# Order of the opening's loads, products without a reader, and query loads two pairs sooner in an attention and two-stage MLP kernel

## The chip, the cores and the metric

The kernel runs on one core of a Trainium2 chip. The metric is the device time of one execution in microseconds (us). TensorE (PE) multiplies, VectorE (DVE), ScalarE (ACT) and GpSimd (POOL) work on what it leaves in PSUM and on data in SBUF, and SyncE (SP) hands out the DMA transfers.

## The reference

What is computed, cut to what matters: attention of 2 batches with 8 heads, 576 positions and 64 elements a head, where a small network of the relative position adds a bias to the scores, then two stages of matrix products on the 1152 rows that come out.

```python
scores = scale * np.matmul(q, k.transpose(0, 1, 3, 2))
rel = (pos[:, None] - pos[None, :]).astype(np.float32)
psi_rel = np.log1p(np.abs(rel))
psi_i = np.log1p(np.maximum(pos[:, None].astype(np.float32), 1.0))
h = np.maximum((psi_rel / psi_i)[..., None] @ w1 + b1, 0.0)   # 32 hidden
scores = scores + (h @ w2).transpose(2, 0, 1)[None, :, :, :]  # 8 heads
attn = softmax(scores);  x = attn @ v          # x: 1152 x 512
x = ((x @ w_a) * (x @ w_b)) @ w_out            # 512 -> 1536 -> 512
h = x @ w_in                                   # 512 -> 1024
solu = h * softmax(h)
out = (layernorm(solu) * g_ln) @ w_out2        # 1024 -> 512
```

The weights of the two later stages come as float64 and are read as pairs of 32-bit words.

## The kernel before

**Units and pairs.** The attention part goes over nine units of 128 rows of scores: units 0 to 7 are four blocks of 128 positions, each for batch 0 and batch 1, and unit 8 holds the last 64 positions of both batches. A unit has four pairs of heads, so the main loop (lines 614 to 682) runs over 36 pairs, m = 0 to 35, and some steps more to drain. In the turn of pair m PE makes the scores of both its heads (`scores`, L399), then DVE adds the bias and takes the minimum row by row (`biased`, L413: `tensor_tensor_reduce`, shown in the trace as `CUSTOM_DVE_ANT_0 e<-s,bias`; two of them make a pair), ACT takes the exponents (L420), POOL multiplies with the reciprocal of the sum (`shares`, L435). PE transposes the result two pairs later (L441, L452) and multiplies it with the values in the turn after (`values`, L484, into the tile `xx`). At the end of a unit ACT and DVE split `xx` into a high and a low part (`xhi`, `xlo`, L495) for the products of the next stage. Engines run their instructions in the order in which the code issues them; the schedule is written out by hand.

**Queries.** The queries of unit u + 2 are loaded by `fetch` (L257) into a tile `nat_q`, one load for heads 0 to 3 and one for heads 4 to 7 (each two DMA issues, four in unit 8), in pairs p = 2 and p = 3 of unit u (last lines of the loop). The query of the next unit is turned by PE in each pair (`turn`, L276), into the tile of scores `spare` that the second head of the pair has just been given. ACT and DVE read it into `qhi` and `qlo` (L309, L318). For unit 8, POOL clears the tiles ahead of that (`clear_q`, L283), in unit 6's last pair and in unit 7's second.

**Bias.** The bias is made in 36 groups of 16 rows, T = 0 to 35. For each, ACT and DVE make four tiles of relus from a table (`bias_hidden`, L361 and L363; who makes which is the table `HIDDEN`), PE sums them over the hidden elements (`bias_sums`, L371, 16 products into a PSUM tile `bps`), ACT scales the sums into the tile `st` (`bias_out`, L381) and SP sends `st` to the bias tile of the block (L383), of which eight groups make one for 128 rows. Groups 0 to 8 are made ahead of the loop (`N0` is 8), group m + 9 in pair m of the loop.

**Opening.** PE makes the right part of the relu table from `psi_r` (`table`, L207), the offsets of the relus (L214) and the scales of the outputs (L227), then the loop over T = 0 to 7 begins. In it PE also turns the queries of unit 0 and the keys of batch 0 (`piece`, L276; a key piece goes to PSUM as `xx`, `tp_k` or a tile of the scores' pool, and ACT and DVE split it into `khi`, `klo`). The left part of the table is made in T = 6. The keys of a batch come in five pieces through an area `arena`; those of batch 1 are turned in pairs 0, 1 and 2 of the loop.

**Queue.** All loads and the bias transfers stand in SP's queue, in the order of the code. An issue takes SP's time, and a transfer that waits for its data holds up all that stand behind it.

**After.** From pair 28 on the words of the first weights of the next stage are loaded and converted between the attention's last pairs (`first_one`: words, ACT's `single` at L94), and from there PE works on the next stages to the end.

The loads of the opening and of the loop are these lines:

```python
for w in ks[1][:3]:
    fetch(w)
for p in range(-1, 2):
    load_v(0, p)
for w in ks[1][3:]:
    fetch(w)
...
if now and p > 1 and u + 2 < NU:
    fetch(("q", u + 2, p - 2, 0))
```

## Time and profile before

| | us |
|---|---|
| median of 3 runs | 536.64 (536.34 to 538.48) |
| the profiled execution | 536.58 |
| its span in the trace | 534.5 |
| TensorE (PE) busy | 504.0 (94%) |
| VectorE (DVE) busy | 401.3 (75%) |
| ScalarE (ACT) busy | 285.2 (53%) |
| GpSimd (POOL) busy | 143.7 (27%) |

The span runs from the first to the last instruction of the profiled execution; what lies around it is 2.1 us. The busy times are sums over the whole program, in which the attention part with its many small steps (until about 200 us) and the large matrix products behind it differ, so they are read by stretch. A row of the time line gives the start, the duration, the engine (SPq: SP's queue, with the time in which it handed out the issues), the line of the kernel, the operation, what it writes and reads, the shape and how many instructions of that kind follow each other. A bracket says how long the engine sat idle before the row and which engine, tile and line released it.

### The profile page before, as it was taken

Reading aid. Unit: us, or ns where it says so; the run is one execution under the profiler, and the core shown is the slowest. Engines: PE = TensorE matmul, PEld = TensorE weight load, DVE = VectorE, ACT = ScalarE, POOL = GpSimd, SP = SyncE. Lnnn points to the kernel's source line nnn. Section 1 sums busy time; section 2 is a strip of 40 time slices with the busy share of each in tenths; the row PEclk is TensorE's granted clock in tenths of the full one; section 3 lists DMA queues with packets and bytes.
Section 4 is the critical chain, followed back from the end, with each engine's and each line's share of the span. In section 5 each row is a group of like instructions: output and inputs, shape, how many; then the busy total and the mean of one; then the engine's idle time right before and its main releaser. Section 6 shows DMA issues by size and latency. Waiting matters only on the chain.

```text
span 534.5 us, 13462 instructions
## 1 busy us (share of the span) xinstructions
PE 504.0 (94%) x5416; PEld 446.1 (83%) x5416; DVE 401.3 (75%) x873; ACT 285.2 (53%) x617; POOL 143.7 (27%) x216
## 2 busy tenths in 40 slices
PE   7848899999979999999999999999999999999997
PEld 3436777877767799999999999999999988888886
DVE  4848899999967943887998898897875466666561
ACT  5847899999978732655564344422535332322221
POOL 2003333344356740322222122242225230000000
PEclk9968999999999999999999999999999999999999
DMA  5886654444653103535543353353300000000011
GB/s 133 196 174 149 155 115 109 94 105 110 149 135 120 42 2 108 172 121 155 158 155 122 118 157 119 119 158 119 120 0 1 1 0 21 20 21 20 25 35 39
DMA packets 63520, 51.74 MB, mean 97 GB/s; under 512 B 41182, under 2 KB 53731, under 8 KB 63460
## 3 DMA queue, kind: packets, MB, share of 16 engines
q1 hardware_dynamic: 63184, 50.88, 35.1%
q8 instruction: 42, 0.69, 0.5%
q14 instruction: 18, 0.15, 0.1%
q10 hardware_dynamic: 276, 0.02, 0.0%
HBM read 36.73 MB, written 2.36 MB: 73 GB/s over the span
## 4 chain that ended last, share of the span: by engine, by line
PE 74%; DVE 8%; ACT 7%; DMA 5%; issue 4%; SPq 1%; POOL 1%; DVEq 0%; ACTq 0%
PE pm L128 27%; PE po L128 14%; PE py L922 9%; PE ph L862 9%; PE bps L371 5%; PE xx L484 3%; DVE h L363 3%; ACT e L420 3%; DMA nat_q<-in_q_dram 2%; DVE e L413 2%; PE pl L903 1%; PE s L399 1%; PE pt L452 1%; DMA words<-in_moe_w_out_dram 1%; ACT qhi L309 1%
## 5 line engine op out<-in xcount | busy, mean ns | idle before, releaser
L128 PE MATMUL pm<-xhi,abh 128*128 128x384 f32 x240 | 80.2, 334 | 0.0
L128 PE MATMUL pm<-xhi,abl 128*128 128x384 f32 x240 | 80.2, 334 | 0.0
L128 PE MATMUL pm<-xlo,abh 128*128 128x384 f32 x240 | 80.2, 334 | 0.0
L98 POOL TENSOR_SCALAR f<-f 128x512 f32<-128x512 f32 x48 | 41.4, 862 | 141.8 <-ACT f L94 117.3
L435 POOL TENSOR_SCALAR e<-e,rec 128x576 f32<-128x576 f32 x72 | 53.4, 754 | 62.9 <-DVE rec L430 52.2
L420 ACT ACTIVATE e<-e,nm 128x576 f32<-128x576 f32 x72 | 55.9, 776 | 22.4 <-DVE nm L413 11.4
L413 DVE CUSTOM_DVE_ANT_0 e<-s,bias 128x576 f32<-128x576 f32 x72 | 53.7, 747 | 13.8 <-DMA arena<-in_k_dram 5.4
L371 PE MATMUL bps<-h,w2bd 128*32 128x288 f32 x576 | 48.2, 438 | 11.1 <-DVE h L363 6.5
L363 DVE TENSOR_SCALAR h<-tabs 128x576 f32<-128x576 f32 x106 | 48.5, 514 | 1.0 <-PE bps L371 0.8
L128 PE MATMUL po<-gh,oh 128*128 128x384 f32 x144 | 48.5, 337 | 0.6 <-DVE x2s L793 0.6
L128 PE MATMUL po<-gh,ol 128*128 128x384 f32 x144 | 48.4, 336 | 0.0
L128 PE MATMUL po<-gl,oh 128*128 128x384 f32 x144 | 48.4, 336 | 0.0
L128 PEld LDWEIGHTS pm<-xhi,abh 128*128 128x128 f32 x240 | 45.1, 188 | 0.0
L128 PEld LDWEIGHTS pm<-xlo,abh 128*128 128x128 f32 x240 | 45.1, 188 | 0.0
L128 PEld LDWEIGHTS pm<-xhi,abl 128*128 128x128 f32 x240 | 45.1, 188 | 0.0
L110 DVE SCALAR_TENSOR_TENSOR f<-words,f 128x512 int32<-128x512 int32 x48 | 42.9, 895 | 1.6
L147 ACT COPY one<-pm 128x384 f32<-128x384 f32 x36 | 17.2, 479 | 50.2 <-PE pm L128 50.2
L94 ACT ACTIVATE f<-words 128x512 f32<-128x512 f32 x48 | 32.4, 676 | 18.3 <-DMA words<-in_moe_w_out_dram 7.6
L484 PE MATMUL xx<-et,vsb 128*32 128x128 f32 (+1 forms) x1280 | 40.1, 267 | 0.0
L371 PEld LDWEIGHTS bps<-h,w2bd 128*32 128x32 f32 x576 | 20.0, 114 | 23.4 <-issue 8.8
L877 ACT ACTIVATE ev<-ph,small 128x512 f32<-128x512 f32 x18 | 12.2, 684 | 49.7 <-DVE small L874 49.7
L484 PEld LDWEIGHTS xx<-et,vsb 128*32 128x32 f32 x1280 | 34.1, 111 | 5.5 <-issue 0.2
(151 smaller groups left out, 1223.7 us busy)
## 6 DMA issues: line engine op xcount, KB each, us to landing
bias<-st SPq DMA_DIRECT2D x40, 288.0 KB, 3.6
words<-in_moe_w_out_dram SPq DMA_DIRECT2D x20, 512.0 KB, 3.5
words<-in_moe_w_a_dram SPq DMA_DIRECT2D x12, 512.0 KB, 3.5
words<-in_moe_w_b_dram SPq DMA_DIRECT2D x12, 512.0 KB, 3.7
nat_q<-in_q_dram SPq DMA_DIRECT2D x32, 128.0 KB, 3.5
words<-in_moe_w_in_dram SPq DMA_DIRECT2D x8, 512.0 KB, 3.6
arena<-in_k_dram SPq DMA_DIRECT2D x16, 128.0 KB, 4.4
vsb<-in_v_dram SPq DMA_DIRECT2D x16, 128.0 KB, 3.7
```

The costliest lines, as they stand in the source:

```text
L94: nc.scalar.activation(f, words[:, :, 1].bitcast(F32), AF.Abs)
L98: engine.tensor_scalar(f, f, WORD_MAX, WORD_MIN, op0=ALU.min, op1=ALU.max)
L110: nc.vector.scalar_tensor_tensor(out=b, in0=words[:, :, 0], scalar=29, in1=b, op0=ALU.logical_shift_right, op1=ALU.bitwise_or)
L128: nc.tensor.matmul(ps, w, x, start=(i == 0), stop=(i == n - 1))
L363: nc.vector.tensor_scalar(h, win, sc, 0.0, op0=ALU.add, op1=ALU.max)
L371: nc.tensor.matmul(bps[32 * qd:32 * qd + 32, a, 0:SH], w2bd, h[:, a * SH:(a + 1) * SH], start=True, stop=True)
L413: nc.vector.tensor_tensor_reduce(out=halves(e), in0=ps[:, :, 0:SH], in1=halves(bias_t[it][:, h, :]), op0=ALU.add, op1=ALU.min, scale=1.0, ...
L420: nc.scalar.activation(e, e, AF.Exp, bias=nm, scale=-1.0, accum_out=sums[:, h:h + 1])
L435: nc.gpsimd.tensor_scalar(e, e, rec[:, h:h + 1], 1.0, op0=ALU.mult, op1=ALU.mult)
L484: nc.tensor.matmul(px[rows, p, cols], lhsT, rhs, start=(c == 0 and m == 0), stop=(c == NC), skip_group_check=True)
L862: nc.tensor.matmul(ph[u][:, a], x[:, kc, cols], w[:, kc, a * 512:(a + 1) * 512], start=(i == 0), stop=(i == 3 * KD - 1))
L922: nc.tensor.matmul(ps, x[:, c, :], w[:, c, cols], start=(i == 0), stop=(i == 3 * KF - 1))
```

## The change

- The first bias group after which the loop starts, T = 9, gets its relus ahead of the loop and not in pair 0.
- Unit 1's queries, batch 1's keys and batch 0's values are loaded behind the transfer of T = 8 (the ninth); before, the queries stood ahead of T = 5 and the rest ahead of T = 8.
- A function `beside` issues products whose result nobody reads: 5, 2 and 2 of 128 columns in the opening, and 2 of 512 columns ahead of the first scores.
- The left part of the table is made in T = 5 and not T = 6, in a tile of the scores' pool, and ACT copies both its halves; before DVE did.
- The queries of unit u + 2 are loaded in pairs 0 and 1 of unit u.
- In the loop the key pieces of pairs 0 to 2 are turned ahead of the bias sums of the pair.
- The tile `xx` becomes two tiles, one for each parity of the unit; a key piece in it is split by two copies of half the size.
- The clears of unit 8's query tiles take the half that no query is written to.

```diff
-        xx = ps_x.tile([P, 2, 512], F32, tag="x", name="xx")
+        xx = [ps_x.tile([P, 512], F32, tag=f"x{r}", name=f"xx{r}") for r in range(2)]
+        def beside(n, ps, x):
+            for _ in range(n):
+                nc.tensor.matmul(ps, ident, x, start=True, stop=True)
...
+        warm_ps = ps_t.tile([P, 2, 512], F32, tag="t", name="warm_ps")
+        beside(5, warm_ps[:, 0, 0:P], ident)
         halves_r = table(half, UW - half, psi_r, half - 12, ps_s, "s")
...
+        beside(2, warm_ps[:, 0, 0:P], ident)
         nc.scalar.copy(*halves_r[0])
...
         scales()
+        beside(2, warm_ps[:, 0, 0:P], ident)
...
-                    nc.gpsimd.memset(t_.bitcast(F32), 0.0)
+                    nc.gpsimd.memset(t_[:, :, ROWS[1 - m]].bitcast(F32), 0.0)
...
+            if (u, h) == (0, 0):
+                beside(2, ps[:, 0], tb[:, UW - 512:UW])
...
-                st_["x", u] = xx[:, u % 2].rearrange("p (a t) -> p a t", a=HP)
+                st_["x", u] = xx[u % 2].rearrange("p (a t) -> p a t", a=HP)
...
-            if T == N0 - 2:
-                halves_l = table(low, half - low, psi_l, low - 12, ps_t, "t")
+            if T == N0 - 3:
+                halves_l = table(low, half - low, psi_l, low - 12, ps_s, "s")
+                for half_l in halves_l:
+                    nc.scalar.copy(*half_l)
...
-            if T == N0 - 3:
-                for g in range(2):
-                    fetch(("q", 1, g, 0))
         assert done is None and len(order) == 3
-        for half_l in halves_l:
-            nc.vector.tensor_copy(*half_l)
         bias_hidden(N0)
         bias_sums(N0 - 1)
         bias_out(N0 - 1)
-        for w in ks[1][:3]:
-            fetch(w)
-        for p in range(-1, 2):
-            load_v(0, p)
-        for w in ks[1][3:]:
-            fetch(w)
-        for p in range(2, HP):
-            load_v(0, p)
...
         bias_out(N0)
+        for w in [("q", 1, 0, 0)] + ks[1][:4] + [("q", 1, 1, 0)] + ks[1][4:]:
+            fetch(w)
+        for p in range(-1, HP):
+            load_v(0, p)
+        bias_hidden(N0 + 1)
...
-            if m == 0:
-                bias_hidden(T)
...
+            made = [piece(w, room) for w, room in zip(keys_at.get(m, []), "xt")]
             if T is not None:
                 bias_sums(T)
-            made = [piece(w, room) for w, room in zip(keys_at.get(m, []), "xt")]
...
-            if now and p > 1 and u + 2 < NU:
-                fetch(("q", u + 2, p - 2, 0))
+            if now and p < 2 and u + 2 < NU:
+                fetch(("q", u + 2, p, 0))
```

SP's queue at the end of the opening, before: `nat_q_1_0` and `nat_q_1_1` are unit 1's queries, `arena` takes the keys of batch 1, `vtl` and `vsb` the values of batch 0, and `st_5` to `st_9` are the bias groups of these numbers.

```order
L257 DMA nat_q_1_0_340<-in_q_dram 128x4x64 x2
L257 DMA nat_q_1_1_343<-in_q_dram 128x4x64 x2
L383 DMA bias_0_208<-st_5_363 16x8x576
L383 DMA bias_0_208<-st_6_392 16x8x576
L383 DMA bias_0_208<-st_7_414 16x8x576
L262 DMA arena_163<-in_k_dram 128x4x64 x4
L269 DMA arena_163<-in_k_dram 32x4x64 x4
L336 DMA vtl_162<-in_v_dram 64x4x64 x2
L338 DMA vsb_161<-in_v_dram 128x4x64 x4
L262 DMA arena_163<-in_k_dram 128x4x64 x4
L338 DMA vsb_161<-in_v_dram 128x4x64 x4
L383 DMA bias_1_486<-st_8_487 16x8x576
```

The same place of SP's queue now:

```order
L399 DMA bias_0_219<-st_7_419 16x8x576
L399 DMA bias_1_471<-st_8_472 16x8x576
L266 DMA nat_q_1_0_475<-in_q_dram 128x4x64 x2
L271 DMA arena_174<-in_k_dram 128x4x64 x4
L278 DMA arena_174<-in_k_dram 32x4x64 x4
L271 DMA arena_174<-in_k_dram 128x4x64 x2
L266 DMA nat_q_1_1_488<-in_q_dram 128x4x64 x2
L271 DMA arena_174<-in_k_dram 128x4x64 x2
L352 DMA vtl_173<-in_v_dram 64x4x64 x2
L354 DMA vsb_172<-in_v_dram 128x4x64 x8
L399 DMA bias_1_471<-st_9_572 16x8x576
L266 DMA nat_q_2_0_589<-in_q_dram 128x4x64 x2
```

All loads that stood ahead of T = 8 stand behind it, queries and keys ahead of the values, and unit 2's first queries follow T = 9.

SP's queue in the last units, before: `nat_q_8_0` and `nat_q_8_1` are unit 8's queries, `st_33` to `st_35` the last bias groups, `words_0` the first weights of the next stage.

```order
L257 DMA nat_q_7_1_2834<-in_q_dram 128x4x64 x2
L383 DMA bias_4_2820<-st_33_2925 16x8x576 x2
L383 DMA bias_4_2820<-st_34_3022 16x8x576 x2
L383 DMA bias_4_2820<-st_35_3121 16x8x576 x2
L257 DMA nat_q_8_0_3127<-in_q_dram 64x4x64 x4
L257 DMA nat_q_8_1_3222<-in_q_dram 64x4x64 x4
L90 DMA words_0_3306<-in_moe_w_a_dram 128x4x256
```

And now:

```order
L399 DMA bias_4_2842<-st_33_2944 16x8x576 x2
L266 DMA nat_q_8_0_2957<-in_q_dram 64x4x64 x4
L399 DMA bias_4_2842<-st_34_3046 16x8x576 x2
L266 DMA nat_q_8_1_3059<-in_q_dram 64x4x64 x4
L399 DMA bias_4_2842<-st_35_3150 16x8x576 x2
L90 DMA words_0_3325<-in_moe_w_a_dram 128x4x256
```

The two query loads each stand two bias groups sooner, and T = 35 is now the last ahead of the words.

DVE at the end of unit 0, with what its instructions wait for, before: `xlo` is the low part of the unit's result, `h_0` and `h_2` are relus, `nm` and `e` belong to the pair's bias step.

```order
L466 COPY et_1_1221<-pt_1_1175 128x8x64 [waits DVE_49,PE_49]
L318 SCALAR_TENSOR_TENSOR qlo_1_0_1058<-s_7_1148,qhi_1_0_1057 128x128 [waits Activation_49]
L495 TENSOR_TENSOR xlo<-xx,xhi 128x4x128 [waits PE_49]
L363 TENSOR_SCALAR h_0_1231<-tabs 128x576 [waits DVE_49]
L363 TENSOR_SCALAR h_2_1235<-tabs 128x576 [waits DVE_49]
```

And now:

```order
L484 COPY et_1_1243<-pt_1_1197 128x8x64 [waits DVE_49,PE_49]
L334 SCALAR_TENSOR_TENSOR qlo_1_0_1083<-s_7_1170,qhi_1_0_1082 128x128 [waits Activation_49]
L513 TENSOR_TENSOR xlo<-xx_104,xhi 128x4x128
L379 TENSOR_SCALAR h_0_1253<-tabs 128x576 [waits DVE_49]
L379 TENSOR_SCALAR h_2_1257<-tabs 128x576 [waits DVE_49]
```

`xlo` stands at the same place in DVE's order and has lost its wait for PE.

## Rows read from the trace of the kernel before

**Rows 1.** Busy time by stretch: us; PE, PEld, DVE, ACT, POOL; clock; DMA; GB/s

```profile
30.00:35.00 5.00, 1.96 (x14) 1.17 (x15) 2.99 (x9) 3.18 (x7) 0.00 (x0) 0.50 0.44 94
155.00:160.00 5.00, 2.29 (x36) 1.88 (x37) 1.97 (x7) 1.42 (x5) 3.46 (x7) 0.84 0.51 101
200.00:300.00 100.00, 99.39 (x730) 98.57 (x730) 79.76 (x131) 50.94 (x98) 21.32 (x26) 1.00 0.44 138
```

**Rows 2.** Time line (start, duration), PE and DVE in pairs 28 to 30

```profile
155.09 0.75 DVE L413 CUSTOM_DVE_ANT_0 e<-s,bias 128x576 f32<-128x576 f32 x1
...
158.00 0.84 PE L276 MATMUL s<-ident,nat_q 64*128 64x64 f32 x4 [2.56 <-DMA nat_q<-in_q_dram]
...
158.87 0.76 DVE L413 CUSTOM_DVE_ANT_0 e<-s,bias 128x576 f32<-128x576 f32 x1 [2.95 <-PE s L276]
...
162.58 0.76 DVE L413 CUSTOM_DVE_ANT_0 e<-s,bias 128x576 f32<-128x576 f32 x1 [1.71 <-PE s L399]
...
162.83 0.29 PE L276 MATMUL s<-ident,nat_q 64*128 64x64 f32 x4
...
165.48 0.76 DVE L413 CUSTOM_DVE_ANT_0 e<-s,bias 128x576 f32<-128x576 f32 x1 [0.17 <-PE s L399]
```

**Rows 3.** Time line of SP's queue ahead of pair 28

```profile
143.75 8.98 SPq L383 DMA_DIRECT2D bias<-st  x6
152.83 6.14 SPq L257 DMA_DIRECT2D nat_q<-in_q_dram  x8
```

**Rows 4.** Time line, ACT and PE in pairs 30 and 31

```profile
165.89 0.72 ACT L94 ACTIVATE single<-words 128x512 f32<-128x512 f32 x1
...
170.36 0.28 PE L441 MATMUL s<-ident,e 64*128 64x64 f32 x2 [1.15 <-POOL e L435]
```

**Rows 5.** Time line, DVE in pair 4

```profile
56.41 0.76 DVE L413 CUSTOM_DVE_ANT_0 e<-s,bias 128x576 f32<-128x576 f32 x1 [1.76 <-PE s L276]
```

**Rows 6.** Time line, SP's queue and PE around pair 8

```profile
67.86 1.10 SPq L257 DMA_DIRECT2D nat_q<-in_q_dram  x2
...
73.22 0.34 PE L276 MATMUL s<-ident,nat_q 64*128 64x64 f32 x4 [0.95 <-DMA nat_q<-in_q_dram]
```

**Rows 7.** Time line, DVE and ACT at a unit's end; DVE's waits, 50 to 215 us

```profile
88.28 0.69 DVE L495 TENSOR_TENSOR xlo<-xx,xhi 128x512 fp32r<-128x512 f32 x1 [0.47 <-PE xx L484]
...
90.60 0.78 ACT L420 ACTIVATE e<-e,nm 128x576 f32<-128x576 f32 x1
...
DVE xlo L495 <- PE xx L484: 2.8, 6, 0.5
```

**Rows 8.** Time line, PE and ACT to 11 us; L371's products (ns least/median/most)

```profile
2.43 2.53 PE L207 MATMUL table<-psi_r 1*32 1x346 f32 x16 [2.43 <-DMA psi_r<-in_w_dram]
...
6.94 2.91 PE L371 MATMUL bps<-h,w2bd 128*32 128x288 f32 x16 [0.41 <-DVE h L363]
...
9.99 0.74 ACT L381 ACTIVATE st<-bps,rp 128x576 f32<-128x576 f32 x1 [1.21 <-PE bps L371]
...
L371 PE MATMUL bps<-h,w2bd x16: 660/687/689, 6.9 to 9.2; 128*32 128x288 f32 x16
...
L371 PE MATMUL bps<-h,w2bd x65: 406/406/431, 12.8 to 20.0; 128*32 128x288 f32 x65
```

**Rows 9.** Time line, ACT, DVE and PE in pairs 0 to 2

```profile
24.46 0.74 ACT L381 ACTIVATE st<-bps,rp 128x576 f32<-128x576 f32 x1
...
31.02 0.76 DVE L413 CUSTOM_DVE_ANT_0 e<-s,bias 128x576 f32<-128x576 f32 x1 [5.35 <-DMA arena<-in_k_dram]
...
36.13 0.69 PE L276 MATMUL xx<-ident,arena 64*128 64x64 f32 x8
...
39.37 0.75 DVE L413 CUSTOM_DVE_ANT_0 e<-s,bias 128x576 f32<-128x576 f32 x1
...
45.56 2.10 PE L371 MATMUL bps<-h,w2bd 128*32 128x288 f32 x16
```

**Rows 10.** The page's DMA issues: count, KB each, median us from issue to landing

```profile
arena<-in_k_dram SPq DMA_DIRECT2D x16, 128.0 KB, 4.4
```

More of the change, by code (lines that the diff above doesn't have):

```diff
@@ L275, in turn @@
                 for r in rows:
[L276 removed]
+                    nc.tensor.transpose((ps[r] if ps is xx else ps[:, r])[:, at + i * HF:at + (i + 1) * HF], nat[ROWS[r], h].rearrange("p s d -> p (s d)"), ident[ROWS[r], ROWS[r]])
         def room_q(u, g, m):
@@ L297, in k_views @@
         def k_views(b, g, c, ps, at):
+            if ps is xx:
+                turned = [t_[:, at:at + HG * HF] for t_ in xx]
+                if c < NK:
+                    heads = slice(g * HG, (g + 1) * HG)
+                    return [(*(t_[:, b, heads, c * P + r * HF:c * P + (r + 1) * HF] for t_ in (khi, klo)), turned[r].rearrange("p (h t) -> p h t", h=HG)) for r in range(2)]
+                hi, lo = (t_[:, b, :, NK * P:SH].rearrange("p (g i) t -> p i g t", g=2) for t_ in (khi, klo))
+                return [(hi, lo, turned[b].rearrange("p (i g t) -> p i g t", i=HG, g=2))]
             turned = ps[:, :, at:at + HG * HF]
```

5 lines of the change are left out of this document (2 added, 3 removed).

## The prediction

> **What bounds the kernel now.** First the busy times by stretch [rows 1]: columns are the busy time of each engine in the stretch, then the granted clock, the DMA share, GB/s. From 200 us on TensorE (PE) is full, and the work there only waits for the attention part to end; a microsecond saved before 200 us ends the program a microsecond sooner. So the forecast is a sum over places ahead of that where something waits. The time line then gives them: a row's bracket says how long its engine sat idle and who ended it. Five places touch the change: the last units [rows 2 to 4], pair 4 [rows 5], pair 8 [rows 6], the unit boundaries [rows 7], and the opening [rows 8 to 10]. Pairs of heads are counted m = 0 to 35, T counts the groups of 16 bias rows; fast pairs in between are bound by VectorE (DVE) or ScalarE (ACT), nothing of which changes.
>
> **The last units, the largest term.** Pair 28 needs the queries of unit 8 on PE, in the same tile of scores that DVE reads next. DVE starts the pair at 155.09 and should start its second half about 0.76 us later; it sat idle 2.95 us and began at 158.87, because PE waited 2.56 us for nat_q [rows 2]. The transfer is late because it is issued late: SP handed out both query loads of unit 8 in one go from 152.83, behind the last bias transfers [rows 3]. The change issues the first of them two pairs, some 8 us, sooner, right behind T = 33, the first of the three groups that SP handed out from 143.75 [rows 3]: from about 144.85 us, two issues later at 0.55 us (two took 1.10, [rows 6]). Its own four issues and the 5.36 us that such a load took from issue to PE's start there (67.86 to 73.22) put it at about 152, 3 us before it is needed. So the wait goes entirely, not in part. [...] From PE's query transposes to the next pair's first DVE row took 158.00 to 162.58 = 4.58 us there, but 162.83 to 165.48 = 2.65 us one pair later, with the clock back. Without the wait the transposes stand at 155.4, the next pair begins at 155.4 + 2.65 = 158.05 and not at 162.58: 4.5 us. Late next would be DVE or ACT with the pair's own work; but pair 29, with the same work, ran from 162.58 to 165.48 = 2.9 us on all engines together, and 155.09 + 2.9 is 158.0 too.
>
> Then GpSimd (POOL): the clears of the last queries, four each time, are halved. The second time they stand ahead of the shares for which PE waited 1.15 us [rows 4]. That wait is the most that this can give, nothing the least, if a clear's fixed part rules; I take 0.5. The words of the first weights are the counterweight: they now wait for the landing of T = 35's bias, issued just before 152.83 [rows 3], near 157 by the 4.4 us of a key load [rows 10], and land as much later, near 161.4; ACT took them up at 165.89 [rows 4], which comes 4.5 us sooner, at 161.4. It costs nothing by this count and up to 1.1 us if they land late. **Last units: -5.0 (from -3.9 to -5.6).**
>
> **Pair 4.** The same wait: DVE idle 1.76 us for the transposes of unit 2's queries [rows 5]. They were fetched in pair 2 and are now in pair 0, behind T = 9's transfer; in SP's order that comes after 26 loads, from about 26.2 us on (below) at 0.55 us each, so near 41, and they land by 47 for a need at 56.41 - 1.76 = 54.65. Nothing else stands late there: DVE's relus follow at once. **-1.8 (from -1.6 to -2.0).**
>
> **Pair 8.** PE waited 0.95 us [rows 6], but DVE was behind by only part of that; I take half. **-0.45 (0 to -0.95).** Later boundaries show no such wait, so for pairs 9 to 27 the sooner loads are worth nothing.
>
> **Unit boundaries.** The change splits the tile xx in two. DVE's xlo no longer waits for PE's next products: 0.47 us before it [rows 7], six times. But ACT is as full there: its next exponent at 90.60 shows no idle time before it, so most of a DVE gain runs into ACT. I take 0.11 of the 0.47, six times. **-0.7 (0 to -2.8).**
>
> **The opening, first part.** The clock of the first microseconds is read from the products themselves: the first sixteen products of the bias sums took 687 ns each, from 12.8 us on the same took 406 [rows 8]. So it is at the lower level until somewhere near 10 to 12 us. Nine idle products are added there. Price: the table's products, two rounds of 346 columns, took 2.53 us; 128 columns are 2.53 / 2 x 128 / 346 = 0.47 us at that level, 0.28 at the upper by 406 / 687. Five start when the identity exists, by my estimate a microsecond ahead of the table's 2.43, and end at 1.4 + 5 x 0.47 = 3.75: 1.3 us late. Four more are 1.9 us, less the 0.41 that PE idled before the first sums: the worst case is 1.3 + 1.9 - 0.4 = +2.8. The best is set by ACT, which idled 1.21 us before its first output [rows 8] and hardly at all in the ten microseconds after: -1.2, if the products raise the clock by about 6 us. I take **+0.4**, below the middle, since PE then works without a break from 1.4 us instead of 2.4.
>
> [...]
>
> **The opening, second part.** ACT's last outputs: two copies of the left table come to ACT from DVE, each narrower than half an output (0.74 us, [rows 9]), so under 0.37, and half of the two in idle time; so T = 8's output, ended at 24.46 + 0.74 = 25.20, ends at 25.55. Now SP: unit 1's queries, keys and the values stood ahead of T = 5 to 8 and share the rings with them; DVE began its first pair only at 31.02, after 5.35 us idle on a DMA [rows 9]; the row names a key load, but the first pair reads the bias, and T = 7's transfer is the last of it. The groups' outputs follow each other at 1.8 us (T = 0 at 9.99, T = 8 at 24.46), so T = 7 is out at 25.2 - 1.8 = 23.4, and in the changed order, with nothing foreign ahead, lands near 27.8 by a key load's 4.4 us; then the first half of pair 0 starts near 28.3, when the scores are done; the two long idle products ahead of them (four times 0.28 each at the upper level) lie in PE's wait. But the second half needs unit 1's queries, now issued behind T = 8: 25.6 + 0.6 = 26.2, and 5.36 us to PE's start as above: 31.55, against 31.02 + 0.7 = 31.7 before. Equal. Four key loads follow at 0.55 us each; the last, issued at 28.9, lands 4.4 us later [rows 10]: 33.3. PE then turns the keys (0.69 for the first eight of sixteen at the lower clock, some 1.1 in all) and sums T = 9 (2.10 at that clock). From the end of the sums, at 36.1, where the key turns began, to DVE's next pair it took 39.37 - 36.1 = 3.3 before: 33.3 + 1.1 + 2.1 + 3.3 = 39.8 against 39.37 [rows 9]. The relus of T = 9, moved ahead, are out of the way in both counts. The clock was 0.50 in 30 to 35 us [rows 1] after PE had idled; PE idles as long now. Pairs 1 and 2 give this back, since their key turns now stand in PE's wait for a free score buffer. The second part: **0 (from -1.7, if the clock stays up, to +1.5, if keys land at 5.5 us)**. DVE's saved copies count for nothing, since DVE then waits anyway.
>
> **Sum.** -5.0 - 1.8 - 0.45 - 0.7 + 0.4 + 0 = -7.55 us. The profiled execution took 536.58 us (span 534.5 and 2.1 around it), the median of the runs is 536.64: the same for this purpose. 536.58 - 7.55 = **529.0 us**. All ends together would be 522.3 and 535.4.
>
> **Rivals.** First, the opening pays: products at the lower level without raising it, keys late. +2.8 and +1.5 for +0.4 and 0: 532.9 us. For it: PE is the first engine to work there, and ACT, behind it, has no slack. Against: ACT's idle 1.21 us. 0.16. Second, the clock: up from 6 us and never down around 30 us: -1.2 and -1.7 for +0.4 and 0: 525.7. Against: PE still has little to do between 29 and 33 us. 0.12. Third, the last units find a new bound, the words or POOL, and give 2.5 instead of 5.0: 531.5. For: the words wait for one more transfer. 0.14. Fourth, the sooner loads are issued but held in SP's queue behind bias transfers, and pairs 28 and 4 wait as before: the last units keep 0.5 and pair 4 nothing: 529.0 + 4.5 + 1.8 = 535.3. Against: the order puts them four transfers further ahead. 0.05. Fifth, slower: 26 loads behind T = 8 on eight completion lanes, each issue waiting for the load eight before it. At 4.4 us it holds (26 / 8 x 4.4 = 14 us, done by 40; the values are wanted only after 45.56, [rows 9]). From about 9 us a landing it decides: keys at 47 and not 41, each later pair behind; at 10 us the keys of pairs 0, 1 and 2 come 5.6 us late each in turn, some 11 us in all: 540 us. Nothing in the trace lands so late; 4.4 is the keys' median. 0.03.
>
> **How the numbers follow.** The forecast has 0.50. A measurement of this kernel tells 0.5%, 2.7 us, from no change: the line lies at 533.9. The forecast, the second and third rival and nearly all of the first lie below: faster 0.90. The fourth and the first's tail: same 0.07. The fifth: slower 0.03. The range 525.3 to 533.0 takes in the first and third rival's centres and half of the second, and leaves 2 in 10 out.
>
> **What would show it.** In the changed trace: no idle bracket from nat_q at PE in pairs 4, 8 and 28, and no clock under 1.00 near 158 us; pair 28 to 29 about 3 us long, pair 32 some 5 us nearer to pair 28 than before; no wait before xlo; the first output of the bias near 10 us; DVE's first pair near 28.3 and pair 1 within 1.5 us of 39.4. It is wrong if SP shows the query loads of unit 8 still issued after T = 35, if ACT waits for words in pair 29, or if pair 1 begins after 41 us.

## The result and the profile after

The changed kernel takes **531.53 us** (median of 5 runs, 530.36 to 532.78) against 536.64 us before, so 5.1 us less; over all runs of both the ratio is 0.9895, 95% interval 0.9864 to 0.9926. That is in the range and on the side that was forecast (529.0; 525.3 to 533.0). The profiled executions are 531.99 and 536.58 us, 4.6 us apart; their spans are 530.2 and 534.5, 4.3 us apart, and it is in these that the steps are compared. Where the time went and where it came back is read from the start of each pair's bias step on VectorE. The table has the start of the pair's first row, before and after, out of the time line.

| pair | before | after | difference |
|---|---|---|---|
| 0 | 31.02 | 31.12 | +0.10 |
| 1 | 39.37 | 41.50 | +2.13 |
| 3 | 50.07 | 52.39 | +2.32 |
| 4, second half | 56.41 | 56.89 | +0.48 |
| 9 | 76.91 | 77.19 | +0.28 |
| 27 | 151.88 | 151.35 | -0.53 |
| 29 | 162.58 | 157.40 | -5.18 |
| 31 | 168.88 | 165.69 | -3.19 |
| 32 | 175.27 | 171.01 | -4.26 |
| 35 | 185.67 | 181.42 | -4.25 |

The opening loses 2.1 to 2.3 us and pair 4 gives 1.85 back. From there to pair 9 it is another 0.2, and from pair 9 to 27, with the unit boundaries, 0.8. Pair 28 gives 4.6; pair 29 takes 0.35 and pair 30 1.6 of it; pair 31 gives 1.1. From pair 35 to the end both take the same 348.8 us.

**The last units.** The time line of SP's queue in the changed kernel (start, time of the issues, line, what is loaded, count), answering to [rows 3]:

```profile
143.22 1.17 SPq L399 DMA_DIRECT2D bias<-st  x2
144.49 2.66 SPq L266 DMA_DIRECT2D nat_q<-in_q_dram  x4
147.25 2.11 SPq L399 DMA_DIRECT2D bias<-st  x2
149.46 2.65 SPq L266 DMA_DIRECT2D nat_q<-in_q_dram  x4
152.21 1.83 SPq L399 DMA_DIRECT2D bias<-st  x2
157.38 0.37 SPq L90 DMA_DIRECT2D words<-in_moe_w_a_dram  x1
```

Unit 8's first queries are issued at 144.49 and not at 152.83. VectorE, pairs 28 to 32 of the changed kernel, answering to [rows 2], and the clock of the same stretch as in [rows 1]:

```profile
154.56 0.75 DVE L431 CUSTOM_DVE_ANT_0 e<-s,bias 128x576 f32<-128x576 f32 x1
155.31 0.74 DVE L431 CUSTOM_DVE_ANT_0 e<-s,bias 128x576 f32<-128x576 f32 x1
157.40 0.76 DVE L431 CUSTOM_DVE_ANT_0 e<-s,bias 128x576 f32<-128x576 f32 x1
...
160.65 0.76 DVE L431 CUSTOM_DVE_ANT_0 e<-s,bias 128x576 f32<-128x576 f32 x1 [0.34 <-PE s L417]
...
165.69 0.74 DVE L431 CUSTOM_DVE_ANT_0 e<-s,bias 128x576 f32<-128x576 f32 x1
...
171.01 0.74 DVE L431 CUSTOM_DVE_ANT_0 e<-s,bias 128x576 f32<-128x576 f32 x1
```

```profile
155.00:160.00 5.00, 4.91 (x134) 4.18 (x130) 4.53 (x15) 4.29 (x14) 3.79 (x8) 1.00 0.47 135
```

Pair 28's second half follows the first at once, pair 29 comes 2.84 us after pair 28 (7.49 before), and the granted clock is 1.00 where it was 0.84 (before, it is 0.50 from 158.35 to 161.76 us, just behind TensorE's wait for nat_q, and 1.00 after that). But from pair 30 to 31 it is now 5.04 us, where it was 3.40. ScalarE and TensorE there, answering to [rows 4]:

```profile
162.54 0.68 ACT L94 ACTIVATE single<-words 128x512 f32<-128x512 f32 x1 [1.51 <-issue]
165.13 0.40 PE L417 MATMUL s<-khi,qhi 64*128 64x288 f32 x2 [1.51 <-DVE qlo_True L334]
```

ScalarE stands idle 1.51 us ahead of the first words of the next stage ("issue": nothing that the profile shows ended the wait), and what stands behind on it, pair 30's exponent and the split of the queries, is late by as much for TensorE. Pair 31 itself takes 5.32 us and not 6.39, since TensorE's wait for POOL's shares [rows 4] is gone.

**The opening.** TensorE to 12 us in the changed kernel, then ScalarE's first and last output (answering to [rows 8, 9]):

```profile
1.35 2.50 PE L176 MATMUL warm_ps<-ident 128*128 128x128 f32 x10 [1.35 <-POOL ident masks.py:199]
3.78 2.53 PE L212 MATMUL table<-psi_r 1*32 1x346 f32 x16
...
6.73 1.22 PE L176 MATMUL warm_ps<-ident 128*128 128x128 f32 x4
...
8.43 1.22 PE L176 MATMUL warm_ps<-ident 128*128 128x128 f32 x4
9.58 2.05 PE L387 MATMUL bps<-h,w2bd 128*32 128x288 f32 x16
```

```profile
11.87 0.74 ACT L397 ACTIVATE st<-bps,rp 128x576 f32<-128x576 f32 x1 [1.11 <-PE bps L387]
...
27.05 0.78 ACT L397 ACTIVATE st<-bps,rp 128x576 f32<-128x576 f32 x1
```

The nine short products take 4.9 us of TensorE (2.50 + 1.22 + 1.22), the sums start at 9.58 and not at 6.94, the first output at 11.87 and not at 9.99, and T = 8's at 27.05 and not at 24.46. Behind it, around pair 0:

```profile
28.40 1.98 PE L176 MATMUL s<-tabs,ident 128*128 128x512 f32 x4 [1.52 <-DVE klo L330]
...
32.78 0.34 PE L285 MATMUL s<-ident,nat_q 64*128 64x64 f32 x4 [1.40 <-DMA nat_q<-in_q_dram]
```

The two long products wait for the scores' buffer and then hold the first scores for 1.98 us; the second half of pair 0 waits for unit 1's queries until 32.78 in any case (e2 below).

### The profile page after: what moved, and what is told of

Read it like the earlier page. It is cut to its first block, busy times and chain, and to the rows that moved or that the text cites. A ratio compares the mean times of both kernels' runs of the same rounds, so it can differ in the third digit from the quotient of the medians.

```text
span 530.2 us, 13526 instructions
## 1 busy us (share of the span) xinstructions
PE 508.7 (96%) x5438; PEld 449.1 (85%) x5438; DVE 400.3 (76%) x874; ACT 285.3 (54%) x622; POOL 142.4 (27%) x216
## 3 DMA queue, kind: packets, MB, share of 16 engines
q1 hardware_dynamic: 63184, 50.88, 35.1%
## 4 chain that ended last, share of the span: by engine, by line
PE 72%; ACT 11%; DVE 7%; issue 5%; DMA 3%; SPq 1%; POOL 1%; DVEq 0%; ACTq 0%; POOLq 0%
PE pm L128 27%; PE po L128 14%; PE py L932 10%; PE ph L872 10%; ACT e L438 4%; DVE h L379 4%; PE bps L387 3%; PE xx L502 3%; ACT st L397 2%; PE pl L913 1%; PE s L417 1%; ACT qhi L325 1%; ACT h L377 1%; DMA words<-in_moe_w_out_dram 1%; DVE qlo L334 1%
## 5 line engine op out<-in xcount | busy, mean ns | idle before, releaser
L387 PE MATMUL bps<-h,w2bd 128*32 128x288 f32 x576 | 49.3, 434 | 2.0 <-DVE nm L431 2.0
L110 DVE SCALAR_TENSOR_TENSOR f<-words,f 128x512 int32<-128x512 int32 x48 | 42.5, 886 | 1.6
L502 PE MATMUL xx<-et,vsb 128*32 128x128 f32 (+1 forms) x1280 | 42.2, 263 | 0.0
L502 PEld LDWEIGHTS xx<-et,vsb 128*32 128x32 f32 x1280 | 35.6, 110 | 6.1 <-issue 0.2
L109 DVE SCALAR_TENSOR_TENSOR f<-words,f 128x512 int32<-128x512 int32 x48 | 34.5, 719 | 1.3
```

The source lines that it names most:

```text
L109: nc.vector.scalar_tensor_tensor(out=b, in0=words[:, :, 1], scalar=-0x40000000, in1=b, op0=ALU.bitwise_and, op1=ALU.bitwise_or)
L110: nc.vector.scalar_tensor_tensor(out=b, in0=words[:, :, 0], scalar=29, in1=b, op0=ALU.logical_shift_right, op1=ALU.bitwise_or)
L387: nc.tensor.matmul(bps[32 * qd:32 * qd + 32, a, 0:SH], w2bd, h[:, a * SH:(a + 1) * SH], start=True, stop=True)
L502: nc.tensor.matmul(px[rows, p, cols], lhsT, rhs, start=(c == 0 and m == 0), stop=(c == NC), skip_group_check=True)
```

## The experiments

The times, in us. The ratio refers to runs of the kernel before that were timed beside each kernel (their medians are 536.64, 536.97, 537.13 and 537.31). The last columns are starts of VectorE's pairs in the profiled execution, and the time from pair 30 to 31.

| kernel | median (range) | ratio, 95% | pair 1 | pair 27 | 30 to 31 | pair 35 |
|---|---|---|---|---|---|---|
| changed | 531.53 (530.36 to 532.78) | 0.9895 [0.9864, 0.9926] | 41.50 | 151.35 | 5.04 | 181.42 |
| e1 no short products | 530.58 (530.30 to 532.19) | 0.9887 [0.9870, 0.9905] | 39.40 | 150.04 | 4.85 | 179.93 |
| e2 no long products | 532.21 (531.79 to 533.78) | 0.9917 [0.9900, 0.9934] | 41.34 | 150.83 | 5.37 | 181.20 |
| e3 none of them | 530.10 (529.63 to 531.74) | 0.9880 [0.9861, 0.9898] | 39.48 | 149.60 | 5.82 | 180.44 |
| e12 first two only | 530.65 (529.28 to 531.61) | 0.9862 [0.9810, 0.9915] | 39.54 | 148.76 | 4.47 | 178.25 |
| e4 before, queries | 531.29 (530.84 to 531.68) | 0.9897 [0.9880, 0.9914] | 39.45 | 150.65 | 3.36 | 180.17 |
| e7 e4 and xx in two | 530.21 (528.58 to 531.58) | 0.9868 [0.9841, 0.9895] | 38.72 | 148.42 | 3.23 | 178.14 |
| e6 e7 and half clears | 530.01 (527.51 to 531.02) | 0.9864 [0.9831, 0.9896] | 39.23 | 148.28 | 3.21 | 176.91 |
| e11 e6, one load later | 529.51 (528.32 to 530.91) | 0.9842 [0.9799, 0.9885] | 39.51 | 149.40 | 3.04 | 177.90 |
| e5 words taken later | 532.92 (531.80 to 533.38) | 0.9917 [0.9895, 0.9940] | 41.30 | 151.39 | 5.52 | 181.81 |
| e8 e3 and e5 | 531.01 (530.88 to 531.52) | 0.9887 [0.9863, 0.9910] | 39.68 | 149.55 | 5.14 | 179.61 |
| e9 fetches moved | 529.73 (529.22 to 531.72) | 0.9854 [0.9793, 0.9916] | 40.37 | 150.58 | 3.09 | 179.10 |
| e10 one load later | 530.57 (529.22 to 531.18) | 0.9859 [0.9808, 0.9911] | 40.37 | 151.15 | 4.64 | 180.70 |

The intervals of nearly all of them overlap, so the times alone rank few; what a step costs is read from the pairs.

### The products that nobody reads: e1, e2, e3, e12

Theory: the short ones cost what they take and bring no clock; the long ones stand in a wait. Rival: they pay by the clock.

e1:

```diff
-        beside(5, warm_ps[:, 0, 0:P], ident)
...
-        beside(2, warm_ps[:, 0, 0:P], ident)
...
-        beside(2, warm_ps[:, 0, 0:P], ident)
```

> The changed kernel without the nine products of 128 columns ahead of the first bias sums (nobody reads their result). Theory: they cost more than the clock gives back. T = 0's output ends 1.9 us sooner (ACT's first output starts near 10.0 and not at 11.87), T = 8's output as much sooner, pair 1 starts near 39.6 and not at 41.50, and the program takes 529.6 us where the changed kernel takes 531.5. Rival: they pay by the clock. The first output starts near 10.0, but the products after it run at the lower level until some 12 us as in the kernel before, T = 8's output gains under 0.5 us, and the time stays within 0.5 us of 531.5 or rises.

The first output starts at 10.00, T = 8's at 25.19 (27.05 with them), pair 1 at 39.40, and pair 27 is 1.3 us sooner. The median fell by about 1 us and not by 1.9, within the runs' spread. The theory holds at pair 1 (2.1 us); 0.8 of it is lost again from pair 2 to 3, where the granted clock from 45 to 51 us was 0.72 and T = 11's sums took 2.17 us (0.96 and 1.20 in the changed kernel).

The 2.1 us are those of one execution. e5 and e10 below leave the opening as it is in the changed kernel, and e2 and e9 keep the nine products too: in all five T = 8's output starts at 27.0 to 27.1, and at 25.2 to 25.4 in e1, e3, e8 and e12, which keeps two. But pair 1 starts at 41.30 in e5 and at 40.37 in e10. T = 9's sums, near 36 us, took 2.17 us in the changed kernel and in e5, and 1.52 in e10, where the granted clock fell at 36.5 us and not at 35.3 or 33.6. So the nine products cost 1.6 to 2.0 us at T = 8's output and, by execution, 0.7 to 2.1 us at pair 1.

e2:

```diff
-            if (u, h) == (0, 0):
-                beside(2, ps[:, 0], tb[:, UW - 512:UW])
```

> The changed kernel without the two products of 512 columns ahead of pair 0's first scores. Theory: they hold pair 0's first half, but its second half waits for unit 1's queries anyway, so the first DVE step of pair 0 comes near 29.2 and not at 31.12, the second stays at 33.2, pair 1 within 0.3 us of 41.5, and the time is the same, 531.5 us within 0.5. Rival one: their 1.98 us stand on the path, pair 1 starts near 39.5 and the time is 529.6. Rival two: they keep the clock up; without them PE's rows from 30 to 36 us run at the lower level, pair 1 starts 1 to 1.5 us later and the time is 532.5 to 533.

Pair 0 starts at 29.95 and its second half at 33.33, as expected; pair 1 at 41.34, 0.16 sooner than with them, pair 2 at 46.95, 0.49 sooner. The long products neither paid nor cost much at the pairs. Rival one is out. Of rival two the first half came true: the granted clock from 30 to 36 us was 0.69 without them and 0.94 with them. But T = 9's sums, at 36 us, took 2.17 us in both, and from pair 1 on no pair got later without them. The median is 0.7 us higher, which is within the runs' spread.

e3 is e1 and e2 together:

> The changed kernel without any of the eleven products that nobody reads. Theory: the gain of leaving out the nine short ones and nothing for the two long ones, 529.6 us, pair 1 near 39.6. Rival (the clock pays): at or above 531.5, with PE's rows at the lower level both ahead of 12 us and around 30 us, and pair 1 at or after 41.5.

ScalarE's first and last output and VectorE's pairs 0 and 1 of this kernel:

```profile
10.02 0.74 ACT L393 ACTIVATE st<-bps,rp 128x576 f32<-128x576 f32 x1 [1.61 <-PE bps L383]
...
25.21 0.78 ACT L393 ACTIVATE st<-bps,rp 128x576 f32<-128x576 f32 x1
```

```profile
27.79 0.76 DVE L425 CUSTOM_DVE_ANT_0 e<-s,bias 128x576 f32<-128x576 f32 x1 [0.43 <-DMA bias<-st]
31.45 0.76 DVE L425 CUSTOM_DVE_ANT_0 e<-s,bias 128x576 f32<-128x576 f32 x1 [2.90 <-PE s L281]
39.48 0.75 DVE L425 CUSTOM_DVE_ANT_0 e<-s,bias 128x576 f32<-128x576 f32 x1
```

This is the rest of the change in the opening by itself: the first half of pair 0 is 3.2 us sooner than in the kernel before, released by the bias as forecast, the second half waits 2.90 us for the queries, and pair 1 starts at 39.48 against 39.37. At pair 1 the order of the loads, the relus and the copies are together worth nothing, and the opening's whole loss there is the short products.

e12 keeps the first two short ones alone, in the time in which TensorE waits for psi_r:

```diff
-        beside(5, warm_ps[:, 0, 0:P], ident)
+        beside(2, warm_ps[:, 0, 0:P], ident)
...
-        beside(2, warm_ps[:, 0, 0:P], ident)
...
-        beside(2, warm_ps[:, 0, 0:P], ident)
...
-            if (u, h) == (0, 0):
-                beside(2, ps[:, 0], tb[:, UW - 512:UW])
```

> The changed kernel with only two of the products nobody reads, the first two, which fit ahead of the table while PE waits for psi_r. Theory: they cost nothing and raise no clock in time: the first output of the bias starts at 10.0 as without any, pair 1 near 39.5, 530.1 us. Rival: PE works from 1.4 us on and its clock rises sooner than without them; the first sixteen sums take under 2.5 us and not 2.9, the first output starts near 9.5, 529.6.

TensorE to 13 us in e12:

```profile
1.34 1.23 PE L176 MATMUL warm_ps<-ident 128*128 128x128 f32 x4 [1.34 <-POOL ident masks.py:199]
2.50 2.53 PE L212 MATMUL table<-psi_r 1*32 1x346 f32 x16
...
7.01 2.91 PE L385 MATMUL bps<-h,w2bd 128*32 128x288 f32 x16 [0.95 <-DVE h L377]
...
10.40 1.20 PE L385 MATMUL bps<-h,w2bd 128*32 128x288 f32 x16
```

The sums take 2.91 us as without any product, the first output starts at 10.07. The two cost nothing. That they raise the level sooner is not shown: the granted clock rose at 10.25 us here, and at 9.98 to 12.96 in the eight kernels without any short product.

### The queries, the split and the clears: e4, e7, e6

e4 is the kernel before with one edit:

```diff
-            if now and p > 1 and u + 2 < NU:
-                fetch(("q", u + 2, p - 2, 0))
+            if now and p < 2 and u + 2 < NU:
+                fetch(("q", u + 2, p, 0))
```

> The kernel before with one edit: the queries of unit u + 2 are fetched in pairs 0 and 1 and not 2 and 3. Theory: this alone carries the gain, and the rest of the change takes some of it away. Pair 4 gives 1.85 us, pair 8 0.3, pairs 28 to 32 3.7 (4.6 at pair 28, of which late words take 1.5 back and a POOL wait gives some again): 536.64 - 5.9 = 530.7 us. Rival one: without the halved clears POOL is late in pairs 29 and 31, and the last units give only 2.5: 532. Rival two: the gain needs the later loads of the opening too (pair 4's queries then stand behind 26 loads or bias transfers that are late anyway), pair 4 gives nothing: 532.5.

This one edit gives 5.7 us (536.97 to 531.29) where the whole change gave 5.1. The two totals lie too near to each other to choose by, but the pairs choose: the theory holds, and both rivals are out. Pair 4's second half follows the first after 0.76 us (2.61 before), pair 9 comes 3.88 us after pair 8 (4.34 before), pair 29 2.82 us after pair 28. ScalarE takes the words without a wait here, and the wait for POOL's shares stays:

```profile
160.62 0.70 ACT L94 ACTIVATE single<-words 128x512 f32<-128x512 f32 x1
```

```profile
164.85 0.28 PE L441 MATMUL s<-ident,e 64*128 64x64 f32 x2 [0.95 <-POOL e L435]
```

e7 adds the two tiles for xx, with the key pieces in it split by two copies (the diff is that of the change in `xx`, `piece` and `values`):

```diff
-        xx = ps_x.tile([P, 2, 512], F32, tag="x", name="xx")
+        xx = [ps_x.tile([P, 512], F32, tag=f"x{r}", name=f"xx{r}") for r in range(2)]
...
-                st_["x", u] = xx[:, u % 2].rearrange("p (a t) -> p a t", a=HP)
+                st_["x", u] = xx[u % 2].rearrange("p (a t) -> p a t", a=HP)
```

> The kernel before with the query loads two pairs sooner and the tile xx in two. Theory: the split gives 0.1 to 0.2 us at each of the six unit ends, 0.8 us by pair 27 (from 150.65 with the queries alone to 149.8), and the time is 530.5 where the queries alone gave 531.3. Rival: ACT is as full there and takes it all: pair 27 at 150.6, 531.3 us.

From pair 9 to pair 27 it takes 73.88 us, where e4 takes 75.00: 1.1 us less. Of this 0.2 lies at each of the four unit ends in between, and 0.26 from pair 21 to 22, which is no unit end and stays unexplained. The theory holds (0.1 to 0.2 at an end); the rival (ScalarE takes it all) is out.

e6 adds the halved clears:

```diff
-                    nc.gpsimd.memset(t_.bitcast(F32), 0.0)
+                    nc.gpsimd.memset(t_[:, :, ROWS[1 - m]].bitcast(F32), 0.0)
```

> The same with POOL's clears halved. Theory: PE's wait of 0.95 us for the shares in pair 31 goes, 529.7 us. Rival one: the clears hide nothing else, pair 32 stays as without them, 530.5. Rival two: ACT waits for late words in pair 30 as in the changed kernel (1.3 to 2.3 us), 531 to 531.5.

TensorE's wait for POOL's shares in pair 31, in e7 and then in e6:

```profile
162.56 0.27 PE L448 MATMUL s<-ident,e 64*128 64x64 f32 x2 [1.14 <-POOL e L442]
```

```profile
161.47 0.27 PE L448 MATMUL s<-ident,e 64*128 64x64 f32 x2 [0.17 <-POOL e L442]
```

1.14 us becomes 0.17, and from pair 31 to 32 it is 5.70 us instead of 6.66: 0.96. The mechanism is shown; the median moved by 0.2 only. Behind pair 35 this profiled execution of e7 takes 2.6 us longer than that of e6 (span less pair 35: 351.7 and 349.1). TensorE's wait for VectorE's first products of the next stage (1.90 against 0.88 us, near 209 us) is 1.0 of it. Most of the rest is the clock from 211 to 215 us, in e7 and then in e6 (columns as in [rows 1]):

```profile
211.00:215.00 4.00, 4.00 (x16) 4.00 (x15) 3.93 (x8) 2.42 (x6) 0.97 (x1) 0.57 0.16 42
```

```profile
211.00:215.00 4.00, 4.00 (x25) 4.00 (x24) 3.93 (x8) 2.38 (x5) 0.93 (x1) 1.00 0.42 131
```

With a granted clock of 0.57, behind that wait, TensorE ran 16 products and not 25, 1.4 us of work at the pace of e6. So the medians of these two do not tell the clears' worth.

### Why the words are late: e5, e8, e9, e10

Theory at first: ScalarE stands ahead of the words, so taking them up later should free pair 30.

e5:

```diff
-FIRST = ((-7, -5, -4, -1, 0, 1), ...
+FIRST = ((-7, -4, -3, -1, 0, 1), ...
```

> The changed kernel, where ACT takes up the first words of the next stage half a turn later (and DVE their first step half a turn later). Theory: in the changed kernel ACT stands 1.51 us before pair 30's exponents, because those words land late, and this is what takes back a part of the gain of the last units. Without that wait pair 31 starts near 164.1 and not at 165.69, pair 35 1 to 1.5 us sooner than 181.42, and the time is 530.2 us where the changed kernel takes 531.5. Rival: the conversion then stands in the way one step later, pair 31 is sooner and pair 32 is not (171.0), and the time is 531.5.

e8 is the same edit without any of the products:

> The changed kernel without the eleven products that nobody reads and with the words taken up half a turn later. Theory: the two losses are apart in time and add up: pair 27 at 149.6, pair 31 near 162.4, 528.3 us, under every kernel so far. Rival: one of them covers the other, 530.1 us as without the products alone.

Both failed; e8's 531.01 us lies above its theory and its rival. ScalarE waits no longer, but VectorE does, for POOL, in the same pair (VectorE in e5):

```profile
165.44 0.83 DVE L107 TENSOR_SCALAR single<-single 128x512 int32<-128x512 int32 x1 [2.03 <-POOL single L98]
```

Pair 30 to 31 takes 5.52 and 5.14 us. The edit moved the steps of one chain (ScalarE, POOL, VectorE) together, and the wait came out at the next of them, so it could not tell when the words arrive. It came out nearer to the rival (the conversion stands in the way one step later), but pair 31 itself was no sooner.

When they arrive stands in the trace's packets and landings. The first words are one issue, for which the trace has 16 landings, called parts here; the page counts 16 DMA engines, whose queues are called rings. In the changed kernel fifteen parts have landed at 160.95, which is ahead of ScalarE's 161.03, and the last at 162.39. A packet of 16 KB in queue q8, which the page calls instruction, started at 158.40 and took 2.12 us, when the words' packets had just begun; such a packet is called a fetch here. The trace gives no ring, so that it stood on that of the late part is a reading of these times, which e9 puts to the test. In e1, e2 and e3 it is the same (fetches from 157.10, 157.88 and 156.71; the last part 1.1, 1.7 and 2.4 us behind the fifteenth), and so it is in e5, e8 and e12 (1.7, 2.2 and 0.7 us). In these seven the fetch starts 0.8 to 2.0 us behind the words' issue. In e4, e7, e6 and e11 it comes 2.99, 3.56, 3.03 and 3.02 us behind it, and the last part is 0.03 to 0.08 us behind. These kernels differ in how many products TensorE has run by then. So e9 moves the fetches and leaves the loads alone:

```diff
+        def filler(n, ps):
+            for _ in range(n):
+                nc.tensor.matmul(ps[0:32, 0, 0:64], ident[:, 0:32], ident[:, 0:64], start=True, stop=True)
...
+            if m == 0:
+                fill_ps = ps_t.tile([P, 2, 512], F32, tag="t", name="fill_ps")
+                filler(16, fill_ps)
             if now and u + 1 < NU:
...
+            if m == 0:
+                filler(16, fill_ps)
             made = [piece(w, room) for w, room in zip(keys_at.get(m, []), "xt")]
```

> The changed kernel with 32 more products nobody reads (32x64, half of them ahead of pair 0's query transposes and half behind, where PE waits for loads). They move the places at which PE's instructions are fetched (16 KB each time, on the rings of the loads) by half a fetch, about 3 us at pair 29. Theory: the first words are late in the changed kernel because such a fetch (2.12 us from 158.40) stands on one of the 16 rings that carry them: fifteen parts have landed at 160.95, the last at 162.39. With the fetch elsewhere all have landed within 0.2 us, ACT's 1.51 us ahead of the words is under 0.3, pair 30 to pair 31 takes 3.4 to 3.7 us and not 5.04. If the moved fetch hits the second words, pair 31 keeps a part of it. Pair 1 is at most 1 us later. Rival: the words are late by SP's late issue alone (157.38, behind the landing of T = 35): then nothing changes, 5.0 us from pair 30 to 31.

The DMA view of the 2.3 us from 158.3, in the changed kernel (GB/s in 40 slices, then the queues: packets, MB, share of 16 engines):

```profile
GB/s 0 285 71 71 107 53 71 142 142 71 160 160 89 267 267 321 356 321 321 338 374 338 356 374 356 356 374 338 374 356 374 374 338 356 392 321 356 374 356 410
...
q1 hardware_dynamic: 609, 0.61, 82.2%
q8 instruction: 1, 0.02, 5.7%
```

and ScalarE and TensorE around pair 30 in e9:

```profile
160.19 0.72 ACT L94 ACTIVATE single<-words 128x512 f32<-128x512 f32 x1
```

```profile
163.70 0.28 PE L464 MATMUL s<-ident,e 64*128 64x64 f32 x2 [0.20 <-POOL e L458]
```

5.7% of 16 engines in 2.3 us is one engine for 2.1 us. In e9 that fetch stands at 155.21, ahead of the words (issued at 156.45); all parts land between 159.70 and 160.04, ScalarE waits for nothing, and from pair 30 to 31 it is 3.09 us (3.4 to 3.7 had been expected). The theory holds and the rival is out, with one qualification: SP issued the words 0.9 us sooner than in the changed kernel, of which 0.8 is the earlier pair 28. Late issue alone would not have mattered: fifteen parts were in time in the changed kernel too. The median is 529.73, 1.8 us under the changed kernel's. Not all of that is the words': e9 is 0.8 us ahead at pair 27 already. Its products lie mostly in TensorE's waits for loads, and behind them the granted clock was 1.00 where it was 0.78 in the changed kernel (e9, then the changed kernel):

```profile
36.00:42.00 6.00, 4.33 (x64) 2.70 (x60) 3.42 (x10) 3.28 (x8) 0.81 (x2) 1.00 0.77 174
```

```profile
36.00:42.00 6.00, 4.71 (x49) 2.61 (x46) 2.01 (x5) 2.44 (x5) 0.00 (x0) 0.78 0.80 177
```

T = 9's sums took 1.20 us there and not 2.17, and the level fell at 42.0 us, where it fell at 27.7 to 36.5 in the other thirteen profiled executions. From pair 27 to 35 e9 is 1.55 us shorter than the changed kernel (28.52 and 30.07), and that is the last units' part.

e10 lets T = 35's transfer pass the second query load:

```diff
-            if now and p < 2 and u + 2 < NU:
+            if now and p < 2 and u + 2 < NU and (u, p) != (NU - 3, 1):
                 fetch(("q", u + 2, p, 0))
+            if now == (NU - 3, 2):
+                fetch(("q", NU - 1, 1, 0))
```

> The changed kernel with the second query load of unit 8 one pair later, behind the transfer of T = 35. T = 35 is then issued about 1.1 us sooner, and the words, which wait for its landing, too. Theory: ACT's wait ahead of the words shrinks from 1.51 to about 0.4 us, pair 31 starts 1.1 us sooner (from pair 30: 3.9 and not 5.04 us), 530.5 us. Rival one: SP hands out the later query load in the time that it gained, and the words go out no sooner than 157.2: 5.0 us, 531.5. Rival two: the queries are now late for pair 30, PE idles there on nat_q: 532.

The words go out at 156.24 (157.38 before) and ScalarE doesn't wait. But pair 30 to 31 takes 4.64 us and not 3.9, since TensorE stops in the middle of one line's products:

```profile
163.59 0.53 PE L502 MATMUL xx<-et,vsb 128*32 128x128 f32 x11 [1.22 <-issue]
```

No tile is late there. The fetch behind the one at 151.98 started only at 161.16, 9.2 us later (about 6 us is the mean of the attention part), and took 1.13 us. Between these two TensorE began 437 of its instructions; no other two fetches of the fourteen traces are more than 384 apart, and the mean is 256. That TensorE ran out of instructions fits these numbers; it is argued from them and was not tested apart. Neither the theory's 3.9 us nor a rival's mechanism came out.

e11 is e6 with the second query load of unit 8 only one pair sooner than in the kernel before (the edit of e10):

> The kernel before with the query loads two pairs sooner, but the second of unit 8 only one pair sooner, the tile xx in two and the clears halved. Theory: the words have slack in this kernel already, so the time is that of the kernel with both query loads two pairs sooner, 530.0 us, and the spread of its runs (527.5 to 531.0) stays. Rival: that spread comes from the words, and with their load 1 us sooner the runs gather at 528.

529.51 us, the lowest median, with runs from 528.32 to 530.91: the spread stayed, as the theory had it, so the words' load is not all of its cause. Its ratio of 0.9842 [0.9799, 0.9885] overlaps the changed kernel's: that it beats the changed kernel is likely from its pairs (pair 35 at 177.90, 3.5 us sooner) and not shown by the times.

## Why the prediction was right, point by point

**Pair 28: right in mechanism and size.** Forecast: the wait goes entirely and the next pair starts 2.9 to 3 us later; measured 2.84, and a clock of 1.00 in the stretch. The queries were issued at 144.49 where 144.85 was worked out. e4 shows that the loads alone do it.

**The last units as a whole: -5.0 forecast, -3.7 measured** (pair 28 to 32: 20.18 us before, 16.45 after), just under the small end of -3.9. Pair 28 gave 4.65, where 4.5 was worked out; pair 29 took 0.35 back. The term that was mis-sized is the words. They were put at 161.4 with up to 1.1 us if late. Fifteen of their sixteen parts came at 160.95 and the last at 162.39, and the wait cost 1.6 us. That the key load's median is a price for the last part of a later transfer was the unsound step. This is the third rival's mechanism with half its price. The clears gave 0.96 (e6 against e7) where 0.5 was taken from a wait of 1.15: nearly all of the wait was the clears. The changed kernel's 1.1 in pair 31 is not theirs alone: pair 31 takes 5.7 to 5.8 us in e6, e11 and e9, where the words are in time, and 5.3 here, where they had put it off.

**Pair 4: right** (-1.85 for -1.8), but that nothing else stands late there was not: from its second half to pair 5 it takes 3.79 us and not 3.33, so 0.46 is given back, and up to pair 9 the net is only -0.2. **Pair 8: right** by e4 (-0.46 for -0.45); that half of the wait was taken was a choice, and its coming out so near is luck. **Unit boundaries: right** in the sum (-0.8 from pair 9 to 27 for -0.7), not in its parts: 0.11 at each of six ends was taken, and it is 0.2 at each of three, 0.24 from pair 21 to 22, and nothing at the end in pairs 11 and 12. Of the wait of 0.47 the row in the changed kernel shows nothing left:

```profile
88.29 0.68 DVE L513 TENSOR_TENSOR xlo<-xx,xhi 128x512 fp32r<-128x512 f32 x1
```

**The opening, first part: wrong in size, +0.4 forecast, +1.9 measured** (9.99 to 11.87, and 2.1 at pair 1 by e1). The price of the products was nearly right: 0.50 us each for the first five against 0.47, and 0.61 for the other four. The step that failed is the other end: that steady work from 1.4 us might lift the clock by 6 us and give 1.2 back. That was the author's estimate, and no run shows such a lift. TensorE worked without a break from 1.35, and the two products at 8.43 (four rows of the trace) still took 1.22 us, as the two at 6.73 did; the two at 1.34 us in e12 took 1.23. The granted clock of 1.00 is on record from 11.39 us, and from 11.58 in the kernel before. The sums began 2.6 us later and took 2.05 instead of 2.91 us. That is not the clock but the relus: at 6.94 the sums still had to wait for them, and at 9.58 they were ready. Sixteen sums without such a wait took 2.17 us from 36.16 us on in the changed kernel, with a granted clock of 0.50, and the second sixteen of e8 took the same:

```profile
10.41 2.17 PE L383 MATMUL bps<-h,w2bd 128*32 128x288 f32 x16
```

This was the first rival's mechanism (the products cost and lift nothing), with 0.16.

**The opening, second part: right for the loads, wrong in one place.** e3 has the first half of pair 0 at 27.79 (28.3 forecast) and pair 1 at 39.48 (39.8, and equal to before). T = 8's output is 0.8 us later by the copies, not 0.35. The loads and the bias transfers stand in one queue of the page (q1: 63,184 packets, 35.1% of the 16 engines' time before and after). The eight lanes of the fifth rival are eight semaphores that the 195 issues in the trace before take in turn, 24 or 25 each; the key loads of the changed kernel landed 3.9 us after their issue in the median, so that rival did not come about. The long products did not lie in a wait: they could begin only when the scores' buffer came free, and held the first half for 1.98 us; it cost little, because the second half was later still. Nor did pairs 1 and 2 give anything back: from pair 1 to 3 it took 10.89 us, and 10.70 before. By one of its own signs the forecast was wrong in the opening: pair 1 began after 41 us, at 41.50.

In the span the sum came out at -4.3 us and not at -7.55. Of the 3.3 us between them the opening has 1.9 (+2.3 up to pair 4 for +0.4), the last units 1.3, and pair 5 0.5; the other places gave 0.4 more than was counted. The two large misses lie on the same side, and the total stayed in the range because it reached 4 us above the forecast.

**What stays open:** one execution differs from another of the same kernel by 0.6 to 3.5 us, more than most steps here are worth. Behind pair 35 the fourteen profiled executions take 348.7 to 351.7 us. Nearly all of the spread is one wait of TensorE near 210 us, for VectorE's product `g`, whose other factor ScalarE copies only behind its wait for the words of `w_out`. In e10 and then in e5, ScalarE's row for those words and TensorE's behind the wait:

```profile
210.11 0.66 ACT L94 ACTIVATE f<-words 128x512 f32<-128x512 f32 x1 [1.56 <-DMA words<-in_moe_w_out_dram]
211.78 0.44 PE L128 MATMUL pm<-xhi,first 128*128 128x384 f32 x1 [0.51 <-DVE g L148]
```

```profile
212.36 0.66 ACT L94 ACTIVATE f<-words 128x512 f32<-128x512 f32 x1 [0.62 <-DMA words<-in_moe_w_out_dram]
214.03 0.44 PE L128 MATMUL pm<-xhi,first 128*128 128x384 f32 x1 [1.65 <-DVE g L148]
```

TensorE began its run of products up to that wait at 202.67 and at 203.79 us, so the words come 7.44 us behind its begin in e10 and 8.57 in e5: 1.13 us later, and the wait is 1.14 us longer. Less this wait (0.51 to 1.90 us) thirteen of them take 348.1 to 348.2 us, and e7, with its clock of 0.57, 349.8. So up to 1.4 us of a difference between two kernels here can lie in a load that none of the edits was about. Why its words land at different times stays open.

## What to carry to other kernels

Issue a load by when it is needed and not by when its tile is at hand: one moved line gave as much here as the whole change (5.7 and 5.1 us), since the transfer's wait of 2.56 us stood ahead of work that other engines wanted; from 155 to 162 us the granted clock was 0.76 with that wait, and 1.00 in e4 and in the changed kernel. Idle products cost here what of their time did not fit into a wait (in the opening 1.9 of 4.9 us; nothing for the first two in e12), and what they are to buy has to be seen in the duration of the products that follow. When a transfer of many parts is a microsecond late, look at its last part: here it landed 1.44 us behind the fifteenth, with a fetch of 2.12 us beside it, and all sixteen landed within 0.34 us in e9, where the fetch stood ahead of them.

## What was not expected of the hardware

- **A fetch stood beside each late part of the words.** The page of the changed kernel has 43 packets, 0.70 MB, in queue q8, all of 16 KB. That they bring TensorE's instructions is read from their number: in each of the fourteen traces one comes for every 255 to 256 of its instructions on the mean (in the changed kernel 10,876 products and weight loads and 94 waits), about every 6 us in the attention part and every 23 us behind it. Most took 0.9 to 1.3 us; those that met the words' load 1.4 to 2.4, and the load's last part landed 1.1 to 2.4 us behind the others (changed, e1, e2, e3, e5, e8; 0.7 in e12, whose fetch took 0.98).
- **The clock's rise did not follow the work of the opening.** With the same products up to 10.4 us, the second sixteen sums took 1.74 us in the kernel before, and in e4 and then e1:

```profile
10.40 1.28 PE L371 MATMUL bps<-h,w2bd 128*32 128x288 f32 x16
```

```profile
10.40 1.86 PE L383 MATMUL bps<-h,w2bd 128*32 128x288 f32 x16
```

  and 1.20 in e12 above: the level rose at another moment in each execution (granted clock from 11.6 us in the kernel before, 10.7 in e4, 11.8 in e1, 10.3 in e12). The nine products did not bring it forward: with them and 8 us of unbroken work the sums from 9.58 us on still took 687 ns each in the median, as those from 6.94 us did before. It rose at 11.3 to 13.2 us in the five kernels with the nine, and at 10.0 to 13.0 in the eight without any.
